# First step of a fused recurrent-attention and MLP kernel: its first loads reordered on one queue, one product moved to GpSimd, an accumulator cleared by TensorE, and the level-six scaling split

## The chip, the cores and the metric

The program runs on one core of a Trainium2 chip, as one launch. Five engines with queues of their own work side by side: TensorE (PE; its weight loads are listed as PEld), VectorE (DVE), ScalarE (ACT), GpSimd (POOL) and SyncE (SP), which only issues transfers here. ScalarE can issue transfers too. An engine takes its instructions in the order in which they were written and waits on semaphores of the others. The metric is the device time of the whole launch in microseconds (us); less is better.

## The reference

Attention with a decaying state (RWKV-6), for 4 sequences, 8 heads, 768 tokens and 48 channels a head, all in fp32:

```
state = 0                                   # per head, 48 x 48
for t in range(768):
    y[t]  = r[t] @ (state + outer(u * k[t], v[t]))
    state = w[t][:, None] * state + outer(k[t], v[t])
```

The outputs of all heads make a row of 384 for each of 3072 tokens, x. Then

```
h  = x @ w_in                               # 384 -> 2048
g  = h * erf(softplus(h))
out = g @ w_out                             # 2048 -> 384
```

## The kernel before

**Tiling.** A step takes two sequences (NJ = 2) and a chunk of 128 tokens (C) for all 8 heads; there are 12 steps, and two sequences' steps alternate with the other two's. Heads are paired (NP = 4 pairs a sequence), two heads of a pair on partitions 0 to 47 and 64 to 111, so r, k and w of a step are tiles of 128 partitions by 8 (JP) by 128 tokens. In the first step the 8 are split into two halves of 4, one for each sequence; a "half" below is such a half.

**The recurrence as products.** A chunk is cut into two runs of 64 tokens (HC), and within these the decay is applied in six levels (LOG). Level L pairs blocks of 2^(L-1) tokens: `level_products` (products at L701) multiplies k of the left blocks by r of the right blocks, `take_level` and `take_blocks` (L711, L718, L732) put the result into the score tile `own`, and `scale` (L357 for the first step by halves, L364 for others) multiplies r of the right and k of the left blocks by the decay totals of their block. The totals are w at level one; each further level's are products of pairs, made on GpSimd (L386). Level one is taken from `rk1`, a copy of r and k in which every other token has been multiplied by u (`multiply_u`: L408 and L412 on VectorE, L425 and L428 on ScalarE, L417 and L421 on GpSimd), so that a token's own term gets u. Its result goes through L967 with the mask `first`.

**The end of a step.** k is transposed (L1012) and copied to `kT` (L1015); `from_own` (L745) multiplies scores by v into the PSUM accumulator `y`; `state_part` (L818) makes k times v, which goes to `middle` (L1025, L1026); `through_state` (L771) adds r times the state to `y`. Then the MLP starts (L1231, hidden products), interleaved with the levels of the next step.

**What fills the first step.** All of this stands in `attend_first`. TensorE has six products on the identity matrix at the start (`stay_warm`, L1056), two more after each half of level one, and one of 384 columns on zeros after each of levels two to five (`keep_busy`, L1065). `y` is cleared by VectorE at the very start (L1608).

**What sets the order.** The order on each engine is written by hand; nothing is scheduled. Loads are issued on SP in the program's order. Their start is further set by touches: a copy of a single element into the buffer to be loaded, which waits for the work named (L211 on ScalarE for the second step's r and k; L274 on GpSimd for pieces of w_in; L995 on GpSimd for the second step's w). GpSimd's own pace is set by `wait_for` (L962), a copy of one element that waits until VectorE has scaled that level. The weights w_in and w_out are given in fp64: their words are loaded, turned to fp32 by ScalarE (L289, L297), shifted by VectorE (L306) and joined by GpSimd (L319); these conversions lie between the steps' own work.

**The first loads before.** u goes on ScalarE's queue (L196). SP issues r and k of half 0 (L197), r of half 1 (L198), k of half 1 (L199), w of half 0 (L200), w of half 1 (L201) and the masks (L202).

## Time and profile before

| | |
|---|---|
| Median of 3 runs | 571.74 us (571.04 to 572.32) |
| The profiled execution | 571.11 us |
| Its span in the profile | 569.3 us, 16709 instructions |
| Granted TensorE clock | 0.999 |
| VectorE's first work on loaded data | 5.00 us from the span's start |
| Level-six scales of the first step end | 19.60 us |
| First product of the MLP (L1231) starts | 26.44 us |

The profile shows one execution. Times of instructions are counted from the span's start, and the launch's time has 1.8 us outside the span. In a timeline a line gives start, length, engine, source line, operation, what is written and read, the shapes, and in brackets the idle time of the engine before it with what released it. Where several instructions are merged, "x2" gives their number and the length is that of all. An instruction that overlaps the one before it on its engine is listed with its full length, so the distance between two starts is shorter than a length. In a list of waits a line gives who waited, for whom, the sum in us, how often, and the longest.

### The profile page before, as it was taken

Reading aid. Unit: us, or ns where it says so; the run is one execution under the profiler, and the core shown is the slowest. Engines: PE = TensorE matmul, PEld = TensorE weight load, DVE = VectorE, ACT = ScalarE, POOL = GpSimd, SP = SyncE. Lnnn points to the kernel's source line nnn. Section 1 sums busy time; section 2 is a strip of 40 time slices with the busy share of each in tenths; the row PEclk is TensorE's granted clock in tenths of the full one; section 3 lists DMA queues with packets and bytes.
Section 4 is the critical chain, followed back from the end, with each engine's and each line's share of the span. In section 5 each row is a group of like instructions: output and inputs, shape, how many; then the busy total and the mean of one; then the engine's idle time right before and its main releaser. Section 6 shows DMA issues by size and latency. Waiting matters only on the chain.

```text
span 569.3 us, 16709 instructions
## 1 busy us (share of the span) xinstructions
PE 561.7 (99%) x7318; PEld 500.2 (88%) x7318; DVE 449.6 (79%) x508; ACT 359.2 (63%) x495; POOL 245.7 (43%) x264
## 2 busy tenths in 40 slices
PE   8999999999999999999999999999999999999997
PEld 6788886688998998998998998898899899989997
DVE  8774886999899898799789689689688487477730
ACT  4668787655458858747756765766676771589500
POOL 3775481632885883383484175176073000000000
PEclk9999999999999999999999999999999999999999
DMA  8794762350435325155145236235332201000000
GB/s 272 241 355 161 249 200 86 151 162 3 147 80 174 109 74 155 33 166 164 31 143 181 39 123 200 39 112 167 48 112 84 47 9 36 2 2 1 28 29 28
DMA packets 54081, 63.24 MB, mean 111 GB/s; under 512 B 35160, under 2 KB 40568, under 8 KB 52984
## 3 DMA queue, kind: packets, MB, share of 16 engines
q1 hardware_dynamic: 53480, 61.98, 34.7%
q8 instruction: 57, 0.93, 0.7%
q10 hardware_dynamic: 528, 0.20, 0.1%
q14 instruction: 16, 0.13, 0.1%
HBM read 52.39 MB, written 8.69 MB: 107 GB/s over the span
## 4 chain that ended last, share of the span: by engine, by line
PE 77%; DVE 7%; issue 3%; POOL 1%; ACT 1%; DMA 0%; ACTq 0%; POOLq 0%
PE m L1353 33%; PE m L1231 27%; PE c L1456 6%; PE pp L701 3%; PE m L1263 2%; PE y L745 2%; DVE in L364 2%; PE y L771 1%; PE pp L818 1%; POOL w_out_sb L1294 1%; DVE h L1196 1%; DVE sums L569 1%; PE c L1353 0%; DVE words L503 0%; DMA xT<-y 0%
## 5 line engine op out<-in xcount | busy, mean ns | idle before, releaser
L1231 PE MATMUL m<-xT,w_in_sb 128*128 128x256 f32 x960 | 214.6, 381 | 0.4 <-ACT h L1240 0.2
L1231 PEld LDWEIGHTS m<-xT,w_in_sb 128*128 128x128 f32 x960 | 180.1, 190 | 25.5 <-issue 0.6
L364 DVE TENSOR_TENSOR in<-in,tot_sb 128x1024 f32<-128x1024 f32 (+1 forms) x55 | 75.3, 1370 | 8.9 <-PE pp L701 6.5
L1240 ACT COPY h<-m 128x512 f32<-128x512 f32 x80 | 46.3, 580 | 52.6 <-PE m L1231 52.2
L1353 PE MATMUL m<-mixed,h 128*128 128x192 f32 x320 | 56.7, 331 | 0.0
L1353 PE MATMUL m<-w_out_sb,h 128*128 128x192 f32 x320 | 56.1, 329 | 0.0
L1353 PEld LDWEIGHTS m<-mixed,h 128*128 128x128 f32 x320 | 51.8, 190 | 0.8
L1353 PEld LDWEIGHTS m<-w_out_sb,h 128*128 128x128 f32 x320 | 52.0, 190 | 0.5
L1353 PE MATMUL m<-w_out_sb,room 128*128 128x192 f32 x288 | 49.7, 326 | 0.0
L1353 PEld LDWEIGHTS m<-w_out_sb,room 128*128 128x128 f32 x288 | 47.3, 190 | 0.1
L503 POOL TENSOR_TENSOR words<-words,own 128x384 f32<-128x384 f32 x21 | 30.4, 1447 | 25.7 <-DVE words L534 13.0
L1191 ACT ACT_TABLE_LOAD x28 | 35.9, 1283 | 8.7 <-DVE h L1196 6.7
L701 PEld LDWEIGHTS pp<-in 48*48 48x48 f32 (+4 forms) x2368 | 30.1, 120 | 10.9 <-issue 6.0
L544 POOL TENSOR_TENSOR words<-words 128x384 f32<-128x384 f32 x28 | 38.7, 1410 | 0.0
L496 POOL TENSOR_TENSOR own<-rest 128x384 f32<-128x384 f32 x7 | 8.1, 1156 | 69.2 <-PE y L745 35.1
L1187 ACT ACT_TABLE_LOAD x28 | 35.9, 1283 | 1.8 <-issue 1.3
L701 PE MATMUL pp<-in 48*48 48x32 f32 (+4 forms) x2368 | 33.9, 206 | 0.3 <-DVE in L364 0.3
L448 POOL TENSOR_TENSOR tot_sb<-tot_sb 128x256 f32<-128x256 f32 (+4 forms) x50 | 31.6, 632 | 3.8
L569 DVE TENSOR_REDUCE sums<-rk 128x16 f32<-128x768 f32 (+2 forms) x31 | 31.4, 1023 | 0.0
L544 POOL TENSOR_TENSOR rk<-words 128x384 f32<-128x384 f32 x28 | 30.6, 1121 | 0.0
L1187 ACT ACTIVATE room<-h 128x1024 f32<-128x1024 f32 x28 | 29.6, 1057 | 0.3
L319 POOL TENSOR_TENSOR w_out_sb<-w_out_sb,rest 128x768 int32<-128x768 int32 x8 | 18.1, 2264 | 21.7 <-DVE w_out_sb L311 21.5
(218 smaller groups left out, 1008.1 us busy)
## 6 DMA issues: line engine op xcount, KB each, us to landing
in<-in_rkw SPq DMA_DIRECT2D x8, 1024.0 KB, 5.1
words<-in_moe_w_in SPq DMA_DIRECT2D x16, 384.0 KB, 5.6
words<-in_moe_w_out SPq DMA_DIRECT2D x16, 384.0 KB, 4.6
words<-in_rk_rows SPq DMA_DIRECT2D x8, 768.0 KB, 6.6
w<-in_rkw SPq DMA_DIRECT2D x11, 512.0 KB
v<-in_v SPq DMA_DIRECT2D x12, 384.0 KB, 5.6
out<-o SPq DMA_DIRECT2D x23, 192.0 KB, 4.1
in<-in_rkw SPq DMA_DIRECT2D x7, 512.0 KB, 5.8
```

The lines of the kernel that those rows point to most:

```text
L364: nc.vector.tensor_mul(halves, halves, view(tots[level - 1], 0, [[1, n], [2, nb], [0, half]]))
L448: nc.gpsimd.tensor_mul(new, pair[:, :, 0], pair[:, :, 1])
L503: engine.tensor_mul(to, to, of[:, :, None, :].to_broadcast([P, NEAR // 2 // half, half, D]))
L544: engine.tensor_mul(to[:, i], r[:, half:], k[:, part * rows + i, None].to_broadcast([P, half, D]),)
L569: nc.vector.tensor_reduce(out=to, in_=of, axis=mybir.AxisListType.X, op=ALU.add)
L701: nc.tensor.matmul(to, lhsT=rk(1, n)[rows(e), s0 : s0 + m], rhs=right, start=True, stop=True,)
L1187: nc.scalar.activation(sp_room, chunks[0], AF.Softplus)
L1191: nc.scalar.activation(at, sp_room, AF.Erf)
L1231: nc.tensor.matmul(ps[:, ff, :], lhsT=w_in_sb[:, g * FG + f + ff, kk * P : (kk + 1) * P], rhs=xT[:, kk, :], start=kk == 0, stop=kk == KT - 1,)
L1240: nc.scalar.copy(h[:, f : f + FT, :], ps[:])
L1353: nc.tensor.matmul(to, lhsT=a[:, f], rhs=b[:, f], start=start and f == 0, stop=f == FG - 1, skip_group_check=True,)
L1456: nc.tensor.matmul(to[:, f], lhsT=turns["weights"][b][:, i * FT + f], rhs=turns["tokens"][a], start=a + b in STARTS and not f, stop=True, ...
```

## The change

- The first step's r, k and w come from an array of their own, `in_rkw_first`, in which the data of a half lie together. SP issues r and k of half 0 as one transfer, then u (which leaves ScalarE's queue), w of half 0, r and k of half 1 as one transfer, w of half 1, and the masks.
- For each half, r is multiplied by u and copied on VectorE; k is multiplied by u on GpSimd and its other tokens are copied on ScalarE.
- The work of the two halves is interleaved: level-one products of half 0, scale one of half 0, level-two products of half 0, then GpSimd's first totals of half 0, and the same for half 1, with scale two of half 0 ahead of scale one of half 1 on VectorE.
- VectorE no longer clears `y`. Six products of zeros with 256 columns write into `y` on TensorE instead (`clear_y`), and the products that only kept TensorE busy between the levels go; the six at the start stay.
- The touch for the first piece of w_in stands behind the first totals of half 0 on GpSimd. The transfer of v is written earlier; its place on SP is the same. The totals of levels three to six are each asked for one level earlier.
- In level six, k of both halves is scaled ahead of r of both halves (`scale_last`); the wait on GpSimd and the second step's work behind it follow k. `kT` is copied by heads' side (e) instead of by halves, ScalarE's copy first.

```diff
@@ -193,12 +194,11 @@
         turns["first"] = t5 = t[:].rearrange("p x n t -> p (x n t)").rearrange(
             "p (j x n t) -> p j x n t", j=NJ, x=2, n=NP
         )
-        nc.scalar.dma_start(out=u_sb[:], in_=u)
-        nc.sync.dma_start(out=t5[:, 0], in_=rkw[0][:, 0:2, b0])
-        nc.sync.dma_start(out=t5[:, 1, 0], in_=rkw[0][:, 0, b1])
-        nc.sync.dma_start(out=t5[:, 1, 1], in_=rkw[0][:, 1, b1])
-        nc.sync.dma_start(out=ws[0][:, b0], in_=rkw[0][:, 2, b0])
-        nc.sync.dma_start(out=ws[0][:, b1], in_=rkw[0][:, 2, b1])
+        nc.sync.dma_start(out=t5[:, 0], in_=rkw_first[:, 0, 0:2])
+        nc.sync.dma_start(out=u_sb[:], in_=u)
+        nc.sync.dma_start(out=ws[0][:, b0], in_=rkw_first[:, 0, 2])
+        nc.sync.dma_start(out=t5[:, 1], in_=rkw_first[:, 1, 0:2])
+        nc.sync.dma_start(out=ws[0][:, b1], in_=rkw_first[:, 1, 2])
         nc.sync.dma_start(out=mask_sb[:], in_=masks)
         loaded[0] = t, vt
 
...
@@ -365,6 +365,17 @@
             halves, halves, view(tots[level - 1], 0, [[1, n], [2, nb], [0, half]])
         )
 
+    def scale_last(batch, k):
+
+        half, nb = 1 << (LOG - 1), JP * C // NJ >> LOG
+        t, tots = turns["first"][:, batch], ready[0][1]
+        at, every, of = (NP * C, 1, 1) if k else (half + HC, NC, 2)
+        halves = view(t, at, [[2 * half * every, nb // every], [1, half]])
+        nc.vector.tensor_mul(
+            halves, halves,
+            view(tots[LOG - 1], 2 * batch * nb + of, [[2 * every, nb // every], [0, half]]),
+        )
+
     def plan_totals(s):
 
 
...
@@ -394,23 +405,14 @@
             in_t = loaded[s][0]
             rk1 = att.tile([P, 2, JP, C], FP32, name="rk1", bufs=1)
             ready[s] = (rk1,)
-            parts = 1 if s else NJ
-            def multiply_u(i, x):
-                n = slice(i * JP // parts, (i + 1) * JP // parts)
+            def multiply_u(x):
                 with_u, plain = (
                     [
                         t.rearrange("p n (t two) -> p n t two", two=2)[..., one]
-                        for t in (rk1[:, x, n], in_t[:, x, n] if s else turns["first"][:, i, x])
+                        for t in (rk1[:, x], in_t[:, x])
                     ]
                     for one in (x, 1 - x)
                 )
-                if not s and not (x and not i):
-                    nc.vector.tensor_mul(
-                        with_u[0], with_u[1],
-                        u_sb[:, :, None].to_broadcast([P, NP, C // 2]),
-                    )
-                    nc.vector.tensor_copy(out=plain[0], in_=plain[1])
-                    return
                 if s == 1 and x:
                     for j in range(NJ):
                         of = slice(j * NP, (j + 1) * NP)
...
@@ -428,14 +430,13 @@
                 nc.scalar.copy(plain[0], plain[1])
 
             if s < 2:
-                for i in range(parts):
-                    for x in range(2):
-                        multiply_u(i, x)
-                        yield
+                for x in range(2):
+                    multiply_u(x)
+                    yield
                 return
             yield
             yield
-            multiply_u(0, 0)
+            multiply_u(0)
 
         tots, tot = [], ws[s][:].rearrange("p n t -> p (n t)")
         tot_sb = att.tile([P, JP * (C - NC)], FP32, name="tot_sb")
...
@@ -454,7 +455,7 @@
             ready[s] = rk1, tots, tot
             yield
             yield
-            multiply_u(0, 1)
+            multiply_u(1)
             return
 
         own = att.tile([P, NH, HC], FP32, name="own")
...
@@ -939,56 +940,91 @@
     def attend_first(xT):
 
 
-        for _ in prepare(0):
-            pass
+        rk1 = att.tile([P, 2, JP, C], FP32, name="rk1", bufs=1)
+        ready[0] = (rk1,)
         totals = plan_totals(0)
         c, _, vt, made, S, S_next, ends = parts_of(0)
         t5 = turns["first"]
         own = att.tile([P, NH, HC], FP32, name="own")
         halves = [range(j * NP, (j + 1) * NP) for j in range(NJ)]
         batch = JP * C // 2 // NJ
+        cleared = {"of": 0}
+
+        def multiply_u(i):
+
+            n = slice(halves[i].start, halves[i].stop)
+            for x, engine, copy in (
+                (0, nc.vector, nc.vector.tensor_copy), (1, nc.gpsimd, nc.scalar.copy)
+            ):
+                to, of = (
+                    t.rearrange("p n (t two) -> p n t two", two=2)
+                    for t in (rk1[:, x, n], t5[:, i, x])
+                )
+                engine.tensor_mul(
+                    to[..., x], of[..., x], u_sb[:, :, None].to_broadcast([P, NP, C // 2])
+                )
+                copy(to[..., 1 - x], of[..., 1 - x])
+
+        def clear_y(times=1):
+
+            to = y[:].rearrange("p e q j t -> p (e q) (j t)")
+            zeros = states[1][0][:].rearrange("p n d -> p (n d)")[:, :UNIT]
+            for _ in range(times):
+                nc.tensor.matmul(
+                    to[:, cleared["of"] % NP], lhsT=ident[:], rhs=zeros,
+                    start=True, stop=True, skip_group_check=True,
+                )
+                cleared["of"] += 1
+
+        def wait_for(t, i=1, x=0):
+
+            nc.gpsimd.tensor_copy(out=block_sb[:, 0:1], in_=t5[:, i, x, NP - 1, t : t + 1])
+
         pp = products([P, NE, JP, HC])
-        for half in halves:
-            level_products(pp, by_pair(made), 1, half)
-            stay_warm(2)
+        turns["pp"] = products([P, NE, JP, HC])
+        multiply_u(0)
+        level_products(pp, by_pair(made), 1, halves[0])
+        scale(0, 1, batch=0)
+        level_products(turns["pp"], first_pair, 2, halves[0])
+        clear_y()
+        wait_for(1, 0)
+        totals(1, part=slice(0, batch))
+        stages["l"](0, loaded[0][0][:, 1, JP - 1, C - 1 : C])
+        multiply_u(1)
+        level_products(pp, by_pair(made), 1, halves[1])
+        scale(0, 2, batch=0)
+        scale(0, 1, batch=1)
+        level_products(turns["pp"], first_pair, 2, halves[1])
+        clear_y()
         nc.scalar.copy(first[:], mask_sb[:, 0, :])
-        totals(1, part=slice(0, batch))
-        for j in range(NJ):
-            scale(0, 1, batch=j)
         load_second(t5[:, 1, 0, NP - 1, 1:2])
-
-        def wait_for(t):
-
-            nc.gpsimd.tensor_copy(out=block_sb[:, 0:1], in_=t5[:, 1, 0, NP - 1, t : t + 1])
-
+        nc.sync.dma_start(out=vt[:], in_=v[0])
         wait_for(1)
         totals(1, part=slice(batch, 2 * batch))
-        totals(2, part=slice(0, batch // 2))
+        totals(2)
         nc.vector.tensor_mul(
             own[:], pp[:].rearrange("p e n t -> p (e n) t"),
             first[:, None, :].to_broadcast([P, NH, HC]),
         )
-        behind = {3: (3,), 4: (4, 5), 5: (6,)}
+        scale(0, 2, batch=1)
+        behind = {2: (3,), 3: (4, 5), 4: (6,)}
         for level in range(2, LOG):
-            pp = turns.pop("pp", None) or products([P, NE, JP, HC])
-            for j, half in enumerate(halves):
-                level_products(pp, first_pair, level, half)
-                scale(0, level, batch=j)
+            pp = turns.pop("pp")
             turns["pp"] = products([P, NE, JP, HC])
-            keep_busy(turns["pp"], (DM,))
+            if level > 2:
+                for j, half in enumerate(halves):
+                    level_products(pp, first_pair, level, half)
+                    scale(0, level, batch=j)
+                clear_y(2 if level == 3 else 1)
             (take_blocks if level == MASKED else take_level)(own, pp, level)
             wait_for(1 << level - 1)
-            if level == 2:
-                totals(2, part=slice(batch // 2, batch))
-            else:
-                totals(*behind[level])
+            totals(*behind.get(level, ()))
             if level == 2:
                 stages["b"](0, 0)
                 stages["b"](0, 1)
                 stages["r"](0)
                 second = prepare(1)
                 next(second)
-                nc.sync.dma_start(out=vt[:], in_=v[0])
             if level == 3:
                 stages["l"](1, ready[0][1][level][:, 0:1])
             if level == LOG - 2:
...
@@ -999,23 +1035,21 @@
         pp = turns.pop("pp")
         for j, half in enumerate(halves):
             level_products(pp, first_pair, LOG, half)
-            scale(0, LOG, batch=j)
+            scale_last(j, True)
         take_level(own, pp, LOG)
-        wait_for(HC - 1)
+        wait_for(0, x=1)
         next(second)
+        for j in range(NJ):
+            scale_last(j, False)
 
         kT = att.tile([P, NH, D], FP32, name="kT", bufs=1)
-        kT_by_e = kT[:].rearrange("p (e n) d -> p e n d", e=NE)
         turned = products([P, JP, P])
         turns["next"] = 1 - turns["next"]
         for n in range(JP):
             nc.tensor.transpose(turned[:, n, :], first_pair(1, n), ident[:])
         from_own(0, own, 1)
-        for half, copy in zip(halves, (nc.vector.tensor_copy, nc.scalar.copy)):
-            copy(
-                kT_by_e[:, :, half.start : half.stop],
-                turned[:, half.start : half.stop].rearrange("p n (e d) -> p e n d", e=NE)[..., :D],
-            )
+        for e, copy in ((1, nc.scalar.copy), (0, nc.vector.tensor_copy)):
+            copy(kT[:, e * JP : (e + 1) * JP], turned[:, :, e * EP : e * EP + D])
         stages["h"](0)
         fence()
         stages["h"](0)
...
@@ -1605,7 +1639,6 @@
     mixing = mix_weights()
     next(mixing)
     make_identity(nc, ident[:])
-    nc.vector.memset(y[:], 0.0)
     nc.vector.memset(sums[:], 0.0)
     for t in banks:
         nc.vector.memset(t[:], 0.0)
...
@@ -1632,7 +1665,6 @@
                 for f in range(0, NT, 2)
             ]
         )
-        stages["l"](0, loaded[0][0][:, 1, JP - 1, C - 1 : C])
         for s in range(n_steps):
             xTs[s] = xs.tile([P, KT, UNIT], FP32, name="xT")
             places = iter(range(8))
...
@@ -1778,6 +1810,9 @@
 
     arrays = {
         "in_rkw": rkw.reshape(steps, 2 * EP, 3, NJ * NP, P),
+        "in_rkw_first": np.ascontiguousarray(
+            rkw.reshape(steps, 2 * EP, 3, NJ, NP, P)[0].transpose(0, 2, 1, 3, 4)
+        ),
         "in_v": np.ascontiguousarray(
             v.reshape(B // NJ, NJ, H, n_pairs, P, D).transpose(3, 0, 4, 1, 2, 5)
         ).reshape(steps, P, NJ * H, D),
```

## The prediction

> **What bounds the kernel now.** I read the page's busy times, then who waited on TensorE from 22 us on, then the timeline of the first 24 us engine by engine, because every edit lies there.
>
> ```profile
> PE 561.7 (99%) x7318; PEld 500.2 (88%) x7318; DVE 449.6 (79%) x508; ACT 359.2 (63%) x495; POOL 245.7 (43%) x264
> PE m L1353 <- ACT o L1359: 0.3, 1, 0.3
> PE pp L701 <- DVE in L364: 0.3, 1, 0.3
> PE y L771 <- DVE middle L1026: 0.3, 1, 0.3
> PE m L1231 <- ACT h L1240: 0.2, 1, 0.2
> PE m L1231 <- DMA xT<-y: 0.2, 1, 0.2
> ```
>
> TensorE works 561.7 of 569.3 us, and after 22 us all its listed waits come to 1.3 us. So from the end of the first step on TensorE sets the end, and what the change can win or lose is how much earlier TensorE reaches its last product of that step, the state product L771 (23.18 us). Step 1 can follow: its second scale on VectorE ends at 32.09 (30.86 + 1.23), while the products that need it start at 33.79.
>
> In the first step TensorE mostly works to stay warm, and VectorE carries the chain:
>
> ```profile
> 5.00 0.43 DVE L408 TENSOR_TENSOR rk<-in,u_sb 128x256 f32<-128x256 f32 x1
> 5.35 0.29 DVE L412 COPY rk<-in 128x256 f32<-128x256 f32 x1
> 5.62 0.43 DVE L408 TENSOR_TENSOR rk<-in,u_sb 128x256 f32<-128x256 f32 x1
> 7.09 1.71 DVE L357 TENSOR_TENSOR in<-in,w 128x512 f32<-128x512 f32 x2
> 8.96 1.23 DVE L967 TENSOR_TENSOR own<-pp,first 128x1024 f32<-128x1024 f32 x1
> 10.59 1.29 DVE L357 TENSOR_TENSOR in<-in,tot_sb 128x512 f32<-128x512 f32 x2 [0.41 <-PE pp L701]
> 11.80 1.33 DVE L711 COPY_PREDICATED own<-mask_sb,pp 128x512 f32<-128x512 int32 x1
> 16.70 1.34 DVE L357 TENSOR_TENSOR in<-in,tot_sb 128x512 f32<-128x512 f32 x2
> 18.28 1.32 DVE L357 TENSOR_TENSOR in<-in,tot_sb 128x512 f32<-128x512 f32 x2 [0.24 <-POOL block_sb L962]
> 1.68 4.54 PE L1056 MATMUL m<-ident 128*128 128x256 f32 x12 [1.68 <-POOL ident masks.py:199]
> 19.14 1.16 PE L1012 MATMUL pp<-ident,in 128*128 128x128 f32 x8 [0.59 <-DVE in L357]
> 23.18 0.66 PE L771 MATMUL y<-in,middle 48*48 48x64 f32 x32 [0.28 <-DVE middle L1026]
> ```
>
> Columns: start, length, engine and line; in brackets the idle time before it and its releaser. From 5.00 to 19.60 VectorE rests for 0.41 and 0.24 us and little else.
>
> The last view is what decides: GpSimd and VectorE in step 1.
>
> ```profile
> 41.95 1.05 POOL L448 TENSOR_TENSOR tot_sb<-w 128x512 f32<-128x512 f32 x1
> 42.39 1.70 DVE L364 TENSOR_TENSOR in<-in,tot_sb 128x1024 f32<-128x1024 f32 x1 [0.82 <-PE pp L701]
> 43.08 1.48 POOL L448 TENSOR_TENSOR tot_sb<-tot_sb 128x256 f32<-128x256 f32 x1
> ```
>
> The same VectorE scale alone takes 1.22, and GpSimd's product of 256 columns 0.60. Here the scale stood 0.5 us until GpSimd's instruction ended, and GpSimd's next stood 0.9 us behind the scale. When both multiply two operands out of SBUF, one stands until the other's instruction ends. L967, with one operand in PSUM, ran beside GpSimd at its usual 1.23.
>
> **Part by part.** Durations are from this one execution; times are from the span's start.
>
> Loads. SP still issues six DMAs. The first (512 KB) released ScalarE and VectorE at 5.00 in before; the next 256 KB pieces landed at 5.6 or before, 6.3 and 7.0, so 256 KB take 0.65 us. Now 512 KB of r and k, u, w, then 512 KB: w of half 0 lands at 5.7 instead of 7.0, r and k of half 1 at 6.95 instead of 6.3; the sum of bytes, so the last w and the masks (8.0), stay. u moves from ScalarE's queue behind the first 512 KB. It is 128 pieces of 16 bytes; the nearest row, the 144 packets of ScalarE's queue at 0.9% of 16 engines over 9 us, gives 1.3 us of engine time, 0.1 us over 16. I take 0; the other end is 0.65, a whole 256 KB. The first ScalarE issue (0.45 us) goes, ahead of an idle stretch: 0.
>
> Clearing y. VectorE's 0.91 us at 1.03 goes; VectorE then waits for the first load, until 5.00 as now: 0. Six 256-column products (0.48 us each, from L1056's 2 in 0.5) replace four warming products and four 384-column ones (0.91 each): less work on TensorE, hidden behind VectorE's scales. If that cover went, each would cost 0.48.
>
> Start. Six warming products hold TensorE until 6.22, so level one of half 0 starts at 6.25 instead of 6.44, whatever GpSimd and the loads do before.
>
> VectorE, 5.00 to the level-two masked copy (11.80 now). One multiply and copy pair goes to GpSimd and ScalarE (0.62, from 5.00 to 5.62), and the 0.41 wait behind warming products goes. In their place, laid out by hand with 0.35 per multiply, 0.27 per copy, 0.61 per scale and 0.57 per GpSimd product: r of half 0 at 5.00; GpSimd's k behind it, 5.35 to 5.96; scale one of half 0 at 6.0 (it waits for GpSimd, and w is there); half 1 lands at 6.95, by when GpSimd has begun its totals (6.9 to 7.5), so r of half 1 starts at 7.46, 0.48 late; scale two of half 0 meets GpSimd's k of half 1 (7.95 to 8.56) and starts at 8.52, 0.44 late; scale one of half 1, which must wait for that k, 9.13 to 9.82 (now it ends at 8.80); L967 at 9.74; scale two of half 1 meets GpSimd's level-two totals, 0.27 late, at 11.15; the masked copy starts at 11.76. Now it starts at 11.80. So the 1.03 us are taken back by 1.19 us of standing and by waits for loads and k that fill VectorE's earlier start on level two. Net 0 by this. If nothing collided it would be 1.2 earlier (10.6); if GpSimd took the pair first at 5.00, 0.35 later (12.15).
>
> Here a rule is weighed against a row. L412's copy of 256 takes 0.29 and L408's multiply of 256 takes 0.43. The touch by GpSimd at 6.32 ran into a VectorE copy at 6.64 without making it longer (all three 0.29), so I let copies pass. The Trainium skill (VectorE: DVE Perf Modes, Mode 2×_2P; SBUF — State Buffer, Who interferes with whom) says that a single-source fp32 copy within SBUF uses both read ports and then shuts GpSimd out and is shut out by it. By that rule the sum is the one of the second rival.
>
> Levels three to five are the same instructions and end where they end now (18.0 to 18.2).
>
> Level six. k's halves (0.35 each) go ahead of r's, and the 0.24 us behind GpSimd's touch go, as k's scale reads no cell that it reads. Now the second scale ends at 19.60 and the transposes at 20.30. Then k of half 1 waits for its level-six products and ends at 19.1, and the transposes end at 19.8: 0.5 won. The r scales fill VectorE to 20.0 while it waits for the transposes; only L771 needs them, past 22.
>
> After it. kT is copied by the two engines one after the other in both kernels (0.48 and 0.56), ScalarE first now; L818 waits for both as before. 0.5 arrives at L771.
>
> What is queued behind the new waits: the touch for the w_in words waits on GpSimd behind scale one of half 0 and half 0's totals, so these words are issued at 8.0 instead of 6.79, and step 1's r and k, which wait for scale one of half 1, at 10.1 instead of 9.06. ScalarE's multiply of that r began at 13.76 on its landing; with 1.1 it is 14.9, ends (with its copy) at 16.85, and take_blocks L732, which began at 16.88, is hardly late. Landing past 15.3 it would hold the transposes in k's place; past 16.0 nothing is left of the 0.5. v follows step 1's loads on SP as now; 1 us is hidden before 20. The w of step 1 is issued 1 us earlier, into an idle stretch (15.5 to 16.5 moved nothing).
>
> Sum: 0.5 with VectorE first, 0.1 with GpSimd first, 1.0 without collisions (ScalarE then holds the transposes). I take 0.4. In this execution 571.11 = 569.3 + 1.8 outside the span; 571.11 - 0.4 = 570.7. The median of the runs lies 0.63 higher, so 571.3.
>
> **The rivals.** Collisions miss: GpSimd's products fall into VectorE's copies and PSUM reads. For it: L967 and GpSimd's totals at 9.01 run side by side. Against: six of VectorE's seven multiplies here read two operands from SBUF. Gain 1.0, or 1.2 if ScalarE is on time for the earlier transposes: 570.6.
>
> Copies stand too: r's copy of half 0 stands behind GpSimd's k until 5.92, scale one starts at 6.44, half 0's totals end at 8.4 behind r of half 1, k of half 1 at 9.7 behind scale two; scale one of half 1 follows at 9.8, the masked copy at 12.4 (0.6 late), and level six's 0.5 only makes up for it: 571.7. For it: 0.29 against 0.43 for the same 256 elements says that the copy runs in another way than the multiply. Against: the copy at 6.64.
>
> A load takes its place: step 1's r lands late, ScalarE is late, and k first brings nothing. For it: ScalarE waited 1.24 us for it already. Against: 0.4 us of room to 15.3. Landing 5.8 us after issue (the page's longest median for such a load) is 15.9 to 16.3: 0 to 0.3 lost, 571.9.
>
> Slower, one mechanism: TensorE's clock falls between 7 and 19 us because the warming products go. TensorE was busy 11.07 of these 12 us; then it is about 9. The first L1056 took 0.46 each, later ones 0.25, so there is a slow state. Transposes, L745, L818, L771 and level six's second half (1.1, 0.7, 0.9, 0.7, 0.4) would double: 3.8 less 0.9 beside VectorE, less 0.4: 574.2. It decides once the clock drops before 18. Against: 70% busy from 18 to 20 at a clock of 1.00, and no gap over 0.9 us. The Trainium skill (TensorE: Matmul & The Clock Gate, Part 1) lets the clock fall only after an idle window of about 3.4 us; by that rule this has no chance.
>
> **How the numbers follow.** Collisions as laid out (571.3) 0.45, copies stand too (571.7) 0.18, collisions miss (570.6) 0.18, late load (571.9) 0.12, clock (574.2) 0.07. The range for 8 in 10 goes from 570.2 (1.2 won, less 0.4 of the runs' own spread) to 572.8 (nothing won, u's 0.65 late and that spread). A difference under 0.2%, 1.1 us, can hardly be told from none here. Faster by more: most of the case without collisions and a little of the first, 0.20. Slower by more: the clock, a third of the late load and a little of the others, 0.14. Within: 0.66.
>
> **What would show it.** Right: GpSimd's multiplies by u or VectorE's instructions beside them lengthened by 0.3 to 0.6; the level-two masked copy at 11.6 to 12.2; transposes ending near 19.8; L771's counterpart at 22.6 to 23.0, and the same lead at the end. Wrong: the masked copy by 11.0 (no collisions); the transposes waiting for ScalarE's level-five copies; products of 256 columns over 0.35 us after 7 us; or a lead in the first step that is gone by 60 us.

## The result: 3.5 us slower, and the profile after

The changed kernel takes 575.25 us in the median of 7 runs (573.35 to 577.0), the kernel before 571.74 in 7 runs beside it (570.55 to 572.92). The ratio is 1.0063, with a 95% interval of 1.0042 to 1.0084. The forecast was 571.3, in a range of 570.2 to 572.8.

The profiled execution after took 577.0 us, the slowest of the seven, with a span of 575.2 and a granted clock of 0.982 over it. In the other six runs this clock was 0.988 to 0.997; in the runs of before whose clock is on record it is 0.999 or 1.000. These are the busy times and the clock row on its page. A digit of the clock row is the granted clock of a fortieth of the span (14.4 us) in tenths:

```profile
span 575.2 us, 16699 instructions
PE 567.9 (99%) x7314; PEld 506.1 (88%) x7314; DVE 447.9 (78%) x507; ACT 358.4 (62%) x492; POOL 243.2 (42%) x266
PEclk9589999999999999999999999999999999999999
```

TensorE has four records less and is busy 6.2 us longer (561.7 before). A call of `stay_warm` or `clear_y` stands in the trace as two records; where products are counted below, records are meant. The MLP products have the same busy time in both (214.6 us for the 960 hidden ones), so the 6 us lie elsewhere, and the clock row says where: its second and third digit, 5 and 8, cover 14 to 43 us, and at first TensorE ran there at about half of its clock. Next, the rows of its timeline that matter, to the first MLP product (start, length, line, shapes, pieces merged; in brackets the idle time before and its releaser):

```profile
6.23 0.69 PE L702 MATMUL pp<-rk 48*64 48x64 f32 x32
7.39 0.70 PE L973 MATMUL y<-s,ident 128*128 128x256 f32 x2
8.84 0.69 PE L702 MATMUL pp<-rk 48*64 48x64 f32 x32 [0.75 <-POOL rk L963]
9.99 0.66 PE L702 MATMUL pp<-in 48*62 48x32 f32 x32 [0.46 <-DVE in L357]
12.05 1.02 PE L702 MATMUL pp<-in 48*60 48x32 f32 x32 [0.20 <-DVE in L357]
13.00 2.07 PE L973 MATMUL y<-s,ident 128*128 128x256 f32 x4
15.00 1.72 PE L702 MATMUL pp<-in 48*56 48x32 f32 x64
21.74 1.94 PE L1049 MATMUL pp<-ident,in 128*128 128x128 f32 x8 [0.27 <-DVE in L374]
27.01 1.10 PE L772 MATMUL y<-in,middle 48*48 48x64 f32 x32
28.89 2.93 PE L787 MATMUL y<-y,mixed 128*128 128x256 f32 x6
32.73 2.86 PE L1265 MATMUL m<-xT,w_in_sb 128*128 128x256 f32 x12
```

The same view of before has here, among others, one of the fillers that went (its two records at 13.19), the six products of L787 (L786 there) and the first of the MLP:

```profile
13.19 0.91 PE L1065 MATMUL pp<-s,ident 128*128 128x384 f32 x2 [0.41 <-DVE own L711]
24.32 1.56 PE L786 MATMUL y<-y,mixed 128*128 128x256 f32 x6
26.44 2.86 PE L1231 MATMUL m<-xT,w_in_sb 128*128 128x256 f32 x12
```

L973 is `clear_y`: its two pieces take 0.70 us at 7.39, and four take 2.07 at 13.00. The eight transposes take 1.94 (before 1.16), the six products of L787 take 2.93 (before 1.56). The first MLP product starts at 32.73 in place of 26.44, 6.29 us late. Counted back from the end of the program, the same product in the two traces is 6.3 us late at 49 us and 5.8 at the end, so nothing is lost after the first step. (The half microsecond between is made up at 120 to 150 us by the kernels of the experiments too, so it belongs to that one execution of before.)

VectorE's chain went nearly as laid out:

```profile
4.80 0.43 DVE L963 TENSOR_TENSOR rk<-in,u_sb 128x256 f32<-128x256 f32 x1 [1.02 <-DMA u_sb<-in_u]
5.14 0.71 DVE L966 COPY rk<-in 128x256 f32<-128x256 f32 x1
7.69 0.43 DVE L963 TENSOR_TENSOR rk<-in,u_sb 128x256 f32<-128x256 f32 x1 [0.94 <-DMA in<-in_rkw_first]
8.23 1.10 DVE L357 TENSOR_TENSOR in<-in,tot_sb 128x512 f32<-128x512 f32 x1
11.91 1.32 DVE L712 COPY_PREDICATED own<-mask_sb,pp 128x512 f32<-128x512 int32 x1
21.17 1.20 DVE L374 TENSOR_TENSOR in<-in,tot_sb 128x256 f32<-128x256 f32 x4 [1.08 <-PE pp L702]
```

The level-two masked copy starts at 11.91 (11.76 was forecast, 11.80 is before). The four scales of level six, all merged, start at 21.17, and now VectorE waits for TensorE: the bound of the first step has passed from VectorE to TensorE at half speed.

**What the clock follows.** The trace lists when the granted clock changed: in every run at multiples of 3.413 us from the first rise. In this execution it rises at 5.28, falls to 0.50 at 12.10 and is back at 1.00 at 32.58 us. Here are TensorE's windows between these points (length; busy us and number of products, then the same for weight loads, VectorE, ScalarE, GpSimd; granted clock; share and rate of the transfers), after:

```profile
5.28:8.69 3.41, 2.81 (x71) 1.96 (x69) 2.47 (x8) 0.43 (x1) 2.15 (x5) 1.00 0.62 238
8.69:12.10 3.41, 2.60 (x102) 1.99 (x103) 3.41 (x5) 0.95 (x3) 1.51 (x5) 1.00 0.90 262
12.10:15.52 3.42, 3.42 (x60) 2.53 (x61) 2.87 (x4) 1.44 (x4) 1.29 (x6) 0.50 0.95 365
15.52:18.93 3.41, 3.41 (x110) 2.69 (x110) 2.13 (x4) 1.67 (x5) 0.48 (x3) 0.50 0.75 234
29.17:32.58 3.41, 3.41 (x38) 2.40 (x38) 1.99 (x3) 1.78 (x5) 2.66 (x2) 0.50 0.79 304
```

The clock fell after a window in which TensorE was busy for 2.60 of 3.41 us, with no rest over 0.75 us. It then stayed at half through windows in which TensorE was busy all the time. So neither idle time nor busy time gives the clock. A third measure does: how much of the array is at work. For each product I count rows x columns of the array that it uses, times the columns that it moves, and call 128 x 128 x 256 one full product (one of the twelve at 32.73). A level product of 48 x 56 x 32 is then 0.02, and 64 of them, some 1.1 us of work, are 1.3. Summed over the records of a window, by the share of each record that falls into it:

```
window (us)     TensorE busy   full products   clock of the next window
after
 5.28 -  8.69      82%              8.4              1.00
 8.69 - 12.10      76%              4.9              0.50
12.10 - 15.52     100%              5.0              0.50
15.52 - 18.93     100%              3.9              0.50
18.93 - 22.34      92%              4.1              0.50
22.34 - 25.76      96%              5.1              0.50
25.76 - 29.17     100%              4.9              0.50
29.17 - 32.58     100%              6.8              1.00
before
 8.52 - 11.94     100%              9.3              1.00
11.94 - 15.35      88%              6.4              1.00
15.35 - 18.76      92%              7.0              1.00
18.76 - 22.18      79%              6.4              1.00
```

Windows of only MLP products hold 13.5. The table suggests that the clock is halved after a window with less than about five full products, and restored after one with more. This was found after the result; the runs below test it.

### The profile page after: what moved, and what is told of

It reads as the page before. It is cut to its first block, busy times and chain, and to the rows that moved or that the text cites. A ratio compares the mean times of both kernels' runs of the same rounds, so it can differ in the third digit from the quotient of the medians.

```text
span 575.2 us, 16699 instructions
## 1 busy us (share of the span) xinstructions
PE 567.9 (99%) x7314; PEld 506.1 (88%) x7314; DVE 447.9 (78%) x507; ACT 358.4 (62%) x492; POOL 243.2 (42%) x266
## 4 chain that ended last, share of the span: by engine, by line
PE 92%; DVE 4%; DMA 1%; ACT 1%; issue 1%; SPq 0%; DVEq 0%; ACTq 0%
PE m L1265 35%; PE m L1387 33%; PE c L1490 6%; PE pp L702 6%; PE m L1297 4%; PE y L746 2%; PE y L772 2%; PE pp L819 2%; DMA in<-in_rkw_first 1%; DVE in L364 1%; PE y L973 1%; PE pp L1175 1%; DVE h L1230 1%; PE y L787 0%; PE c L1387 0%
## 5 line engine op out<-in xcount | busy, mean ns | idle before, releaser
L1265 PE MATMUL m<-xT,w_in_sb 128*128 128x256 f32 x960 | 214.6, 381 | 0.3 <-ACT h L1274 0.2
L364 DVE TENSOR_TENSOR in<-in,tot_sb 128x1024 f32<-128x1024 f32 (+1 forms) x55 | 74.9, 1361 | 9.0 <-PE pp L702 6.8
L702 PEld LDWEIGHTS pp<-in 48*48 48x48 f32 (+4 forms) x2368 | 32.1, 126 | 11.1 <-issue 7.0
L702 PE MATMUL pp<-in 48*48 48x32 f32 (+4 forms) x2368 | 36.2, 212 | 0.7 <-DVE in L357 0.7
```

Source lines behind the costliest of these rows:

```text
L364: nc.vector.tensor_mul(halves, halves, view(tots[level - 1], 0, [[1, n], [2, nb], [0, half]]))
L702: nc.tensor.matmul(to, lhsT=rk(1, n)[rows(e), s0 : s0 + m], rhs=right, start=True, stop=True,)
L1265: nc.tensor.matmul(ps[:, ff, :], lhsT=w_in_sb[:, g * FG + f + ff, kk * P : (kk + 1) * P], rhs=xT[:, kk, :], start=kk == 0, stop=kk == KT - 1,)
```

## The experiments

Medians beside these are of the kernel before, run on the same chip: 571.28 us for the first four, 571.26 for the next four, 571.33 for the three after these, and 571.32 for the last. Theories: **rests** (idle time in level one brings the clock down), **array work** (the table above), **level six** (k first costs time of its own), **code fetch** (TensorE's instructions come late; this one arose from the first runs) and its rival, **place** (what looked like late code is a wait of those products themselves).

### Both rests filled, or only the first

```diff
         level_products(turns["pp"], first_pair, 2, halves[0])
         clear_y()
+        stay_warm(2)
...
         scale(0, 1, batch=1)
+        stay_warm(1)
         level_products(turns["pp"], first_pair, 2, halves[1])
```

> The changed kernel with warming products put back in the two rests of TensorE during level one: two after the first product that clears y, one ahead of level two of half 1. Clock theory: the changed kernel is slow because TensorE rests 0.75 and 0.46 us between 8 and 10 us and its granted clock then falls to a half from 12.1 to 32.4 us; with the rests filled the clock stays at 0.998 or more, the MLP's first product starts at 25.8 to 26.4 us as in the kernel before or a little earlier, and the time is 570.5 to 571.7. Collision theory: the loss comes from VectorE and GpSimd standing in each other's way; the filling changes nothing there, and the time stays at 574 to 576.

Measured: 574.44 us (572.95 to 575.99), ratio 1.0052 [1.0036, 1.0069], clocks of 0.994 to 0.997. With only the first added line:

> The changed kernel with the first rest alone filled (two warming products after the first product that clears y). Clock theory, if the gate looks at the sum of TensorE's work over some 3.4 us: the rest that is left, 0.46 and 0.20 us, is about what the kernel before has between 12 and 16 us at full clock, so the time is 570.5 to 571.9. If any rest near 12 us is enough to bring the clock down, it stays at 573 to 576. Collision theory: 574 to 576.

Measured: 575.24 us (574.11 to 577.25), ratio 1.0067 [1.0051, 1.0083]. In its trace the clock stays at 1.00 up to 20.4 us and falls behind a window of 2.9 full products, in which TensorE rests 1.28 us for no wait that the profile shows.

The filling did what it should at its place: with both, the clock stays at 1.00 up to 23.7 us instead of 12.1. But little time came back, as something new shows in the timeline. TensorE with both rests filled:

```profile
14.01 0.28 PE L702 MATMUL pp<-in 48*56 48x32 f32 x3
14.57 1.02 PE L702 MATMUL pp<-in 48*56 48x32 f32 x61 [0.27 <-issue]
18.30 0.38 PE L973 MATMUL y<-s,ident 128*128 128x256 f32 x1 [0.69 <-issue]
21.99 0.73 PE L819 MATMUL pp<-v,kT 64*48 64x48 f32 x22 [0.57 <-DVE kT L1054]
24.92 0.56 PE L819 MATMUL pp<-v,kT 64*48 64x48 f32 x9 [2.19 <-issue]
```

"issue" means that TensorE waited for nothing that the profile shows. The rests stand amid a group whose operands were long there: after 3 of 64, between the two halves of one product, after 22 of 32. Counted in TensorE's records they follow 221, 349 and 476 products, so 127 or 128 lie between two rests. And 128 products with their weight loads are 256 instructions. The page has 57 packets of 16 KB on a queue called "instruction" for 7314 products: again 128 for a packet. The trace gives each packet's time:

```
kernel                     packet on its way (us)   TensorE goes on   rest
both rests filled             12.15 - 13.09            14.57          0.27
                              15.93 - 16.86            18.30          0.69
                              22.63 - 23.57            24.92          2.19
first rest filled             16.81 - 17.71            19.05          1.28
                              23.00 - 23.96            25.40          1.25
before, k first in level six  19.60 - 21.24            22.45          0.31
                              31.07 - 32.05            33.40          0.93
```

In every row TensorE goes on 1.2 to 1.5 us after a packet has landed. The traces of all runs hold 20 such rests of 0.15 us or more up to 42 us, in ten runs. Every one follows 221, 349, 476, 604, 730, 731 or 858 products, whatever product stands there, and ends 1.2 to 1.6 us after a landing. So I read these rests as late code. The long one also empties a window: 20.24 to 23.66 holds 4.6 full products, and the clock falls at 23.66, until 30.5.

### The kernel before without its four warming products

```diff
             level_products(pp, by_pair(made), 1, half)
-            stay_warm(2)
```

> The kernel before without the four warming products after the halves of level one, and nothing else. Clock theory: TensorE then rests between 8 and 10 us here too, the granted clock falls to a half for some multiple of 3.4 us, and the time is 573 to 577. Collision theory: no product by u lies on GpSimd here, and VectorE's wait of 0.41 us behind the warming products goes, so the time is 571.2 to 571.8.

Measured: 571.7 us (570.36 to 576.02), ratio 1.0024 [1.0004, 1.0044]. Seven of twelve executions are at 570.4 to 571.9 with a clock of 0.999 or 1.000, the other five at 573.5 to 576.0, four of them with 0.985 to 0.997. The profiled one held its clock with TensorE busy for only 2.85 us between 8 and 12 us; its windows have 5.3 to 7.4 full products. So the rests alone don't bring the clock down each time. That the kernel now stands just above five, and an execution falls on one side or the other by how the windows lie, fits the array theory, but isn't shown by this run.

### Level six alone

The kernel before with `scale_last` in level six and the copies of `kT` as in the change, nothing else:

```diff
-            scale(0, LOG, batch=j)
+            scale_last(j, True)
...
+        for j in range(NJ):
+            scale_last(j, False)
```

> The kernel before with the level-six part of the change alone: k of both halves scaled ahead of r, and kT copied by e. If this part does what the prediction said, the transposes end 0.5 us earlier and the time is 571.2, with the clock untouched at 0.999. If ScalarE's copies of level five hold the transposes instead, 571.7 as before. If this part brings down the clock, over 573.

Measured: 571.55 us (570.44 to 575.13), ratio 1.0011 [0.9997, 1.0025]. The forecast half microsecond isn't there. Nine executions are at 570.4 to 572.2 with a clock of 0.999 or 1.000, and three at 573.4 to 575.1 with 0.994 to 0.996, so in some executions this part alone goes with a lower clock (none of the 23 of before beside it is under 0.999). In its trace level one starts 0.18 us later than in before, and then:

```profile
18.60 1.16 DVE L374 TENSOR_TENSOR in<-in,tot_sb 128x256 f32<-128x256 f32 x4 [0.40 <-PE pp L712]
19.17 1.06 PE L1024 MATMUL pp<-ident,in 128*128 128x128 f32 x8 [0.41 <-DVE in L374]
```

The transposes start when k of half 0 is scaled, and all eight run one behind the other. That scale waits for the level-six products of its half and ends at 19.02, where the whole scale of half 0 ended at 18.99 in before. So the transposes start at 19.17 (19.14 before) and end at 20.23 (20.30 before), and almost nothing is won ahead of any rest. The first MLP product starts at 26.78 (26.44 before), with a rest of 0.31 us for code amid the products by `kT` and one of 0.93 amid the first MLP products.

### The kernel before with narrow fillers: busy, but little array work

```diff
-                pp[:].rearrange("p e n t -> p (e n t)")[:, :n], lhsT=ident[:],
-                rhs=zeros[:, :n], start=True, stop=True, skip_group_check=True,
+                pp[:].rearrange("p e n t -> p (e n t)")[:, :n], lhsT=ident[:16] if narrow else ident[:],
+                rhs=zeros[:16, :n] if narrow else zeros[:, :n],
+                start=True, stop=True, skip_group_check=True,
```

with `narrow=True` for the four products behind levels two to five.

> The kernel before, with the four zero products of 384 columns behind levels two to five (0.91 us for both records of one) made on 16 rows in place of 128: TensorE is busy as long as before, in the same places, but these products work an eighth of the array. Array theory (the granted clock of a window of 3.41 us follows the rows x columns x moved columns of the window before, and halves where this is under about a third of what the MLP products reach): the window from about 12 to 15.3 us falls from 0.45 to about 0.2 of the dense rate, so the clock is at half from about 15.3 us until the MLP products, over 22 us at least; level five, six, the transposes and the state products take twice as long, the first MLP product comes 2 to 4 us later than 26.44, and the median is 573.0 to 575.5. Rest theory (only idle time counts): clock 1.00 throughout, first MLP product at 26.3 to 26.6, 571.3 +- 0.6.

Measured: 574.73 us (573.24 to 578.32), ratio 1.007 [1.0047, 1.0093]. This decides between rests and array work. First one of the narrow fillers, then the window of before that holds its full one (13.19 above), then the windows of this run's trace, with the same columns as above:

```profile
13.26 0.91 PE L1065 MATMUL pp<-s,ident 16*128 16x384 f32 x2 [0.42 <-DVE own L711]
11.94:15.35 3.41, 3.00 (x129) 2.23 (x121) 3.40 (x5) 2.17 (x6) 1.52 (x5) 1.00 0.77 303
11.48:14.89 3.41, 2.98 (x128) 2.06 (x130) 3.41 (x5) 1.96 (x6) 1.05 (x4) 1.00 0.89 352
14.89:18.31 3.42, 3.42 (x87) 2.21 (x78) 2.56 (x5) 0.92 (x4) 1.58 (x6) 0.50 0.47 128
18.31:21.72 3.41, 2.88 (x68) 1.69 (x69) 1.91 (x4) 2.26 (x6) 0.35 (x2) 0.50 1.02 323
21.72:25.13 3.41, 3.37 (x58) 2.88 (x58) 1.71 (x5) 0.80 (x2) 1.96 (x4) 0.50 0.46 180
25.13:28.55 3.42, 3.13 (x123) 2.77 (x120) 1.13 (x3) 2.08 (x6) 3.38 (x3) 1.00 0.27 45
```

TensorE is busy 2.98 of 3.41 us from 11.48 on, as in before (3.00 from 11.94 on), with the same instructions in the same places up to the fall. Only the rows in use differ: 3.0 full products in place of 6.4. The clock falls at 14.89. It stays at half behind 3.42 of 3.42 us busy (1.8 full products) and comes back behind 5.4. The first MLP product starts at 29.68, 3.2 us late.

### Loads out of the way of the code

Both rests filled, and two loads moved behind the copies of `kT`:

```diff
-            if level == LOG - 2:
-                nc.gpsimd.tensor_copy(out=ws[1][:, 0, 0:1], in_=ready[0][1][LOG - 1][:, 0:1])
-                nc.sync.dma_start(out=ws[1][:], in_=rkw[1][:, 2])
-                stages["l"](2)
...
             copy(kT[:, e * JP : (e + 1) * JP], turned[:, :, e * EP : e * EP + D])
+        nc.gpsimd.tensor_copy(out=ws[1][:, 0, 0:1], in_=kT[:, 0, 0:1])
+        nc.sync.dma_start(out=ws[1][:], in_=rkw[1][:, 2])
+        stages["l"](2)
```

> The changed kernel with both rests filled, and besides the load of step 1's w and the third pair of w_in words put behind the copies of kT (about 22 us in place of 17.3 to 17.8). Fetch theory (TensorE's instructions come in pieces of 128 products' records, each asked for when the piece before is begun, and wait on the DMA engines behind data): the piece that began to land at 22.6 lands about 2 us earlier, the rest of 2.19 us amid the products by kT (L819 in the kernel with both rests filled) goes or falls under 0.6 us, the first MLP product comes at 28 to 29.5 in place of 31.35, and the median falls from 574.4 to 571.5 to 573. Theory of the place (these products wait for a buffer or a copy that the trace does not show): the rest stays at 1.8 to 2.5 us, 574.4 +- 0.7.

Measured: 573.0 us (571.96 to 574.89), ratio 1.0035 [1.0022, 1.0048], 1.4 us better than with the loads in their old place, with clocks of 0.997 to 1.000. Two executions with a clock of 1.000 still took 573.36, the profiled one, and 574.89. TensorE, at the place of the 2.19 us rest and behind it:

```profile
18.23 0.38 PE L973 MATMUL y<-s,ident 128*128 128x256 f32 x1 [0.97 <-issue]
21.92 0.88 PE L819 MATMUL pp<-v,kT 64*48 64x48 f32 x30 [0.57 <-DVE kT L1050]
27.75 0.46 PE L702 MATMUL pp<-rk 48*64 48x64 f32 x16 [1.17 <-issue]
34.09 2.21 PE L1266 MATMUL m<-xT,w_in_sb 128*128 128x256 f32 x9 [0.48 <-issue]
```

The rest amid L819 is gone: its packet started at 19.99 in place of 22.63. The products, their operands and their order are the same, so it wasn't a wait of the place. But the loads, now at 22 us, stand ahead of the next packets, and rests of 1.17 and 0.48 us appear there.

### 64 small products ahead

```diff
-        stay_warm(6)
+        for _ in range(32):
+            ps = ps_m.tile([P, NC, P], FP32, name="m")
+            nc.tensor.matmul(
+                ps[:2, 0, :2], lhsT=sums[:, 0, 0:2], rhs=sums[:, 0, 0:2], start=True, stop=True
+            )
+        stay_warm(5)
```

> The changed kernel with both rests filled, and 32 products of 2 x 2 columns (64 records) at the very start, before the warming products, of which five stay in place of six: nothing else moves, but each piece of instructions now ends 64 records earlier in the program. Fetch theory: the three rests without a releaser move by 64 records: from amid level four of the first step to amid or ahead of level three, from the end of level five to its start, and from L819's 22nd record to the end of level six, just ahead of the transposes; amid L819 there is none. How long they are then I can't say within 1 us each; 572 to 575. Theory of the place: the rest of about 2.2 us stays amid L819, 574.4 +- 0.7.

Measured: 583.06 us (581.09 to 586.96). The edit spoiled its own measurement. The 64 records of 2 x 2 columns took 3.98 us at the clock of the start, 62 ns each, so they moved everything behind them: level one began at 9.80 instead of 6.88, the clock was at half from 20.18 to 33.84, and the first MLP product came at 35.03 instead of 31.35. Against both rests filled this execution lost 2.9 us more behind that point, which wasn't followed up. Only the place can be read from it:

```profile
18.76 0.27 PE L702 MATMUL pp<-in 48*48 48x32 f32 x3
20.02 1.40 PE L702 MATMUL pp<-in 48*48 48x32 f32 x61 [0.98 <-issue]
28.01 1.44 PE L819 MATMUL pp<-v,kT 64*48 64x48 f32 x30
```

The rest from the end of level five now stands after three records of level five's products, and amid L819 there is none, as the code theory has it. The rest that it expected amid or ahead of level three isn't there, and the one ahead of the transposes (1.41 us) is put down to ScalarE by the profile. With both edits:

> Both edits together: 64 records ahead, and w of step 1 and the third pair of words behind the copies of kT. Fetch theory: the piece needed at the end of level six is asked for at about 16 us and lands by 18.5, before the loads; no rest without a releaser over 0.5 us before 22 us, a clock of 1.00 throughout, the first MLP product at 26.0 to 27.5, and 570.5 to 572. Theory of the place: no better than the kernel with both rests filled, 574.4 +- 0.7.

Measured: 582.7 us (582.6 to 583.55), spoiled in the same way. Neither forecast came true; a rest of 1.04 us stands at 20.36, after three records of level five.

### Three loads apart, with and without filled rests

r and k of step 1 go behind the first half's first scale, w of step 1 behind level six's scales, the third pair of words behind the middle state:

```diff
+        load_second(t5[:, 0, 0, NP - 1, 1:2])
         stages["l"](0, loaded[0][0][:, 1, JP - 1, C - 1 : C])
...
-        load_second(t5[:, 1, 0, NP - 1, 1:2])
...
-            if level == LOG - 2:
-                nc.gpsimd.tensor_copy(out=ws[1][:, 0, 0:1], in_=ready[0][1][LOG - 1][:, 0:1])
-                nc.sync.dma_start(out=ws[1][:], in_=rkw[1][:, 2])
-                stages["l"](2)
...
         wait_for(0, x=1)
+        nc.gpsimd.tensor_copy(out=ws[1][:, 0, 0:1], in_=block_sb[:, 0:1])
+        nc.sync.dma_start(out=ws[1][:], in_=rkw[1][:, 2])
...
+        stages["l"](2, middle[:, 0, 0:1], True)
         stages["l"](3, middle[:, 0, 0:1], True)
```

With both rests filled:

> The changed kernel with both rests filled, and three loads moved out of the way of TensorE's instructions: r and k of step 1 behind the first half's first scale (about 7.5 us in place of 10.3), w of step 1 behind level six's first scales (20.4 in place of 17.3), the third pair of w_in words behind the middle state (24 in place of 17.8). Fetch theory: the rest of 0.28 amid level four goes or halves, that of 0.97 after level five (asked for at about 14.2, 3.4 us at the least) falls to 0.4 to 0.9, those of 2.19 amid L819 and of 1.17 ahead of the MLP (in the kernel with the loads behind kT) both go; first MLP product at 26.4 to 27.5, clock 1.00, 570.8 to 572.2. If loads have nothing to do with it: as the kernel with both rests filled, 574.4 +- 0.7.

Measured: 573.34 us (572.9 to 575.27), ratio 1.0039 [1.0027, 1.0051]. The rests amid level four, L819 and ahead of the MLP are gone, one of 0.66 before level six is left. But the window from 16.88 to 20.30 holds 3.6 full products, the clock is at half in the next, and the first MLP product starts at 28.18. The forecasts of a clock of 1.00 and of 570.8 to 572.2 us missed.

The same without the filled rests:

> The changed kernel with the three loads moved, and its two rests not filled. Array theory: the work of the window ahead of 12 us stays at about five full products, so in most executions the clock still falls for 10 to 20 us: 573.5 to 576, clock of the span under 0.997. Theory that late loads and fetches alone explain the loss: 571 to 572.2, clock 1.00.

Measured: 576.57 us (572.17 to 577.77), ratio 1.0086 [1.0063, 1.0109]. The six executions fall into two groups: 572.17 and 572.96 with a clock of 1.000, and 576.51, 576.63, 577.52 and 577.77 with 0.985 to 0.988. The same program thus took about 4.5 us more in the executions in which its clock fell. The profiled execution is one that held it, and so it shows about what the change is worth at full clock, with these loads moved:

```profile
14.63 0.92 PE L702 MATMUL pp<-in 48*56 48x32 f32 x55 [0.69 <-issue]
18.63 0.71 PE L702 MATMUL pp<-in 48*32 48x32 f32 x59 [0.57 <-issue]
19.81 1.09 PE L1047 MATMUL pp<-ident,in 128*128 128x128 f32 x8 [0.47 <-ACT own L733]
23.68 0.66 PE L772 MATMUL y<-in,middle 48*48 48x64 f32 x32
26.96 2.86 PE L1264 MATMUL m<-xT,w_in_sb 128*128 128x256 f32 x12
```

The transposes start at 19.81 (19.14 before) and the first MLP product at 26.96, 0.52 us late, behind 1.26 us of rests for code. Ahead of the transposes TensorE waits 0.47 us for ScalarE's level-five copies (L733), as the prediction named among the signs of being wrong; the run with filled rests waits 0.56 there. The moved loads also cost something: words of w_in that come later delay VectorE, and TensorE waits 0.39 us for a scale of step 1 (L364) at 38.56, which it doesn't in before.

### Fewer records

The kernel with the loads apart and both rests filled, its fillers and clears made of longer products:

```diff
-        stay_warm(6)
+        stay_warm(3, 2 * NC)
...
-        clear_y()
-        stay_warm(2)
+        clear_y(2)
+        stay_warm(1)
...
-                clear_y(2 if level == 3 else 1)
+                clear_y(2 if level == 4 else 1)
```

where `clear_y(2)` is now one product of 512 columns.

> The same, with the filling and clearing done by fewer and longer products: three warming products of 512 columns in place of six of 256, a clear of 512 in place of a clear and one of the two fillers, and one clear of 512 in place of two of 256. The array works as much, in ten records less ahead of level four. Fetch theory: the pieces of instructions end ten records later in the program, so the rest after level five moves to amid level six and is 0.1 to 0.3 shorter; first MLP product at 26.2 to 27.2, 570.5 to 572. If records don't matter: the same as the run with the loads apart, within 0.3.

Measured: 575.88 us (573.38 to 577.36), ratio 1.0071 [1.0053, 1.009]. The forecast of 570.5 to 572 missed. In the profiled execution the first step holds one rest for code, of 0.43 us (amid level four, after 221 products again, not amid level six), a clock of 1.00 throughout, and the first MLP product at 26.96, as expected. But this execution loses 3.4 us between 59 and 85 us, and its span is 573.8:

```profile
61.40 1.27 PE L1267 MATMUL m<-xT,w_in_sb 128*128 128x256 f32 x4 [0.20 <-DMA xT<-y]
64.17 6.24 PE L1267 MATMUL m<-xT,w_in_sb 128*128 128x256 f32 x20 [1.50 <-DMA xT<-y]
```

Here TensorE waits for a transfer of its data, xT, with the words of w_out and the next step's r and k issued beside it (60.31 and 61.49). The window from 61.26 to 64.67 holds 5.5 full products, the most ahead of half clock in all traces, and the clock is at half from 64.67 to 68.08. In three of the other five executions the clock is 0.988 or 0.991.

### One more product in a rest

The kernel with the loads apart and both rests filled, and one product more:

```diff
             scale_last(j, True)
+        clear_y()
```

> The changed kernel with both rests filled and the three loads apart, and one more zero product of 256 columns on the whole array behind level six, in the rest of 0.56 us ahead of the transposes. Array theory: the window from about 17 to 20.3 us, whose work was 3.6 full products of 256 columns (records) in the run with the loads apart, gets two more and passes the five at which the clock stayed; so in nearly all executions the clock is 0.997 or more, and the spread shrinks: 572.0 to 573.3, all executions under 574. What is then left above 571.3 is the rests at the ends of pieces of instructions, 0.7 us, and the half microsecond of later loads. If a fuller window does nothing: 573.3 as before, with executions at 0.994 and above 574.

Measured: 575.23 us (572.29 to 576.04), ratio 1.0062 [1.0043, 1.008]. The forecast of 572.0 to 573.3 with all executions under 574 missed: five of six are above, one of them (574.62) with a clock of 1.000. The added work did its part in the trace: the window from 17.74 now holds 8.1 full products, and the clock is 1.00 up to 34.8 us, with the first MLP product at 27.17. But the time was lost again behind it:

```profile
31.73 0.48 PE L1267 MATMUL m<-xT,w_in_sb 128*128 128x256 f32 x1
34.61 4.33 PE L1267 MATMUL m<-xT,w_in_sb 128*128 128x256 f32 x11 [2.40 <-issue]
38.87 1.08 PE L702 MATMUL pp<-in 48*60 48x32 f32 x64
```

A rest of 2.40 us amid MLP products whose operands had served the ones before. The packet is on its way from 32.12 to 33.03, while the DMA engines are busy all the time (a share of 1.00 between 31 and 33 us). The window of the rest holds 1.8 full products, and the next one runs at half clock: eleven products in 4.33 us, where twelve take 2.86. Together that is 4.3 of the 4.5 us by which this execution ends later than before.

**Over all fourteen traces** (before, after and the twelve runs), 138 windows lie between the first rise and 42 us. All 23 that are followed by half clock hold at most 5.1 full products. Of the 115 followed by full clock, 112 hold 5.2 or more; three hold 4.2, 4.8 and 4.8. Busy time doesn't separate them: windows 66% busy are followed by full clock, windows 100% busy by half. With the best single bound for each measure, 3 windows fall on the wrong side by rows x columns x moved columns, 9 by rows x moved columns, 8 by columns x moved columns, 15 by busy time and 19 by moved columns alone. Only the rows were varied by a run of their own; that columns count as rows do rests on these windows. After 42 us a single window in all traces holds less than 6.5 full products, the one with 5.5 in the run with fewer records, and the clock falls behind it. None of the runs beats the kernel before.

## Why the prediction was wrong, point by point

**The step that failed is "Clearing y".** It took six short products for four warming and four long ones as "less work on TensorE, hidden behind VectorE's scales", at 0. Less work was the loss. With the fillers of before the windows from 8.5 to 18.8 us held 6.4 to 9.3 full products; without them the window to 12.10 held 4.9, and the clock was at half for 20.5 us. The narrow fillers show this in the kernel before, with the fillers' time and order untouched: 3.5 us. In the changed kernel itself, putting work back into both rests kept the clock up to 23.7 us in its trace, but left 3.2 of the 3.5 us, for late code then emptied another window.

**The clock was among the rivals, at 0.07 and 574.2.** Its kind was right and its size nearly (2.5 us lost, 3.5 measured), its chance was not. Two arguments put it down. "70% busy from 18 to 20 at a clock of 1.00, and no gap over 0.9 us" is true but counts busy time, which isn't what counts: the window from 18.76 held 6.4 full products, four of them from the eight transposes. The rule of the Trainium skill (TensorE: Matmul & The Clock Gate, Part 1), by which the clock falls after an idle window of about 3.4 us, doesn't account for this fall, and that it falls only then was the prediction's reading: no rest was over 0.75 us, and the half clock lasted through six windows, five of them over 95% busy. The length of its window agrees with the trace, 3.413 us. What was named as a sign of it, products of 256 columns over 0.35 us after 7 us, came: 0.5 us each at 13.00.

**Level six, 0.5 won: not there.** Alone in the kernel before it changed the time by something between 0.2 us won and 1.4 lost. The term took the transposes to end 0.7 us behind the last scale that they need, as in before. But in before half of them had run by then. With k of both halves ready almost together they need 1.06 us from their start, and the start hardly moves (19.17 against 19.14): 0.07 us won at their end, at most 0.25 net of the later start of level one. At full clock, in the run with the loads apart and rests unfilled, the transposes end at 20.90, where 19.8 was forecast, behind rests for code. The sum had no term for code. In the trace of before, levels three and four take 4.1 us (11.69 to 15.83) for 132 records. By the shortest parts seen, a packet needs about 3.4 us (1.1 from the end of one rest to the start of the next packet, 24.92 to 26.04 with both rests filled; 0.9 to 1.0 on its way; 1.2 to 1.5 until TensorE goes on). That a packet is asked for when the piece before it is begun is read from these times, not shown by a record. If so, by this estimate the pace of before just hides it, and a VectorE that is quicker by more than some 0.7 us in two levels only uncovers TensorE's code.

**Loads.** The first half was right: VectorE starts at 4.80. u cost 0.26 us behind it (ScalarE starts on the data at 4.54, VectorE and GpSimd wait for u until 4.80), between the ends of 0 and 0.65. The second half was forecast at 6.95 and landed at 7.66. That is where the first rest comes from: TensorE waits 0.75 us for GpSimd's k of half 1.

**Collisions.** The copy L966 beside GpSimd's product took 0.71 us, where 0.29 is usual, so copies stand too. The row that I let decide, a touch of one element, was no measure for it. The rule of the Trainium skill that the prediction weighed (VectorE: DVE Perf Modes, Mode 2×_2P; SBUF — State Buffer, Who interferes with whom), by which such a copy takes both read ports and then one of the two engines stands, agrees with the trace: the copy ends at 5.85, 0.15 us behind GpSimd's product. It cost little, for VectorE then waited 0.94 us for the late second half. The scale at 8.23 took 1.10 us beside GpSimd's k of half 1 (0.68 without such company at 9.26), 0.42 where 0.44 was forecast. Net of all, the masked copy at 11.91 against 11.76 was right, and likewise the issues of the words (8.19 against 8.0) and of step 1's r and k (10.19 against 10.1). In part this is luck: r of half 1 starts at 7.69 against 7.46, but behind its late load, and not behind GpSimd's totals.

**The other rivals.** No late load of step 1 held the kernel back by itself, as that rival had it; the loads delay TensorE's code instead. How the loss divides: at full clock the change ends 0.8 to 1.6 us above 571.33 (two executions with the loads apart, whose moved loads cost part of it), and about 4.5 us more are lost in the executions whose clock falls. In the change itself the clock of all seven runs is below that of before. The clock isn't everything, though. Half clock costs at most half of the time spent at it, so at most the span times what the granted clock lacks to 1. For the execution at 574.83 (0.996) that is some 2.6 us, and it lost 3.1. Executions of other runs with a clock of 1.000 reached 574.62 and 574.89; they weren't profiled, and what they lost stays open. What the collisions and the late second half cost apart wasn't run alone.

## What to carry to other kernels

Products that only fill a rest are judged by rows x columns x moved columns in each window of the clock, not by busy time: before taking one away, count that sum by window, and keep well above the sum at which the clock was seen to fall. A chain of small products can be limited by how fast TensorE's code arrives; here 128 of them in less than some 3.4 us left rests. Look for rests without a releaser at every 128th product, and keep large loads from standing ahead of the next piece of code, but count what the moved loads then delay. Before moving a stage's last wait, check how long the work behind it takes from its own first start. When a kernel's runs spread over several us, set the granted clock of each run beside its time before explaining the median.

## What the hardware showed that was not expected

- The clock follows array work: of 138 windows of 3.413 us up to 42 us, all with 5.2 or more full products (of 13.5 in the MLP) are followed by full clock, 23 of the 26 with less by half clock, at 30 to 100% busy. One later window with 5.5 was followed by half clock, and windows with 4.2, 4.8 and 4.8 by full clock, so the bound is not exact.
- Half clock keeps itself up: at half clock a window holds fewer products, so a busy TensorE with small products stayed there for 20.5 us, until L787's full products came.
- TensorE's code comes in packets of 16 KB for 128 products. TensorE goes on 1.2 to 1.6 us after a packet has landed; behind loads a packet started 4.3 us after the rest before it had ended (18.30 to 22.63 with both rests filled), and rests were up to 2.40 us. The Trainium skill (Runtime: NRT & Kernel Launch, Instruction fetch mechanics) gives the size of 16 KiB or 256 instructions, as the trace has it, and calls the crossing mostly hidden, which it is in the kernel before but not in these runs.
- The 64 products of 2 x 2 columns took 62 ns each at the clock of the start, more than twice the 27 ns of a level product at half clock (64 in 1.72 us at 15.00, after). Why isn't shown.
